# Attention logits finished on VectorE from head-major rows read back from DRAM, instead of by selector matmuls on TensorE

## The chip, the cores and the metric

The kernel runs on one core of a Trainium2 chip. The metric is device time in microseconds (us). Every profile is of one execution on the chip. TensorE is called PE in the profile, VectorE DVE, ScalarE ACT, GpSimd POOL; SP is the engine whose queue issues nearly all DMAs (all but two loads of `x` in the trace before).

A ratio of times is the mean time of one kernel's runs over the mean of the other's in the same rounds, so it is not quite the ratio of the medians that stand beside it. Brackets after a ratio are its 95% interval.

## The reference, cut to what matters

Two pairs of layers are applied to one sequence of 2048 tokens of width 1024. The first layer of a pair is sliding-window attention with 32 heads of 32 dimensions, 8 keys per query at a distance of 2 tokens. The second is a gated MLP of width 3584.

```
def _A_ref(x, wqkv, wo):
    B, S, D = x.shape
    H = 32; Dh = D // H
    W, dil = 8, 2
    qkv = (x @ wqkv).reshape(B, S, 3, H, Dh)              # (transposed; cut)
    ...
    logits = jnp.einsum("bhsd,bhswd->bhsw", q, kg) * scale
    logits = jnp.where(mask[None, None, :, :], logits, -1e9)
    attn = _softmax(logits, axis=-1)
    o = jnp.einsum("bhsw,bhswd->bhsd", attn, vg)
    return o.transpose(0, 2, 1, 3).reshape(B, S, D) @ wo

def _B_ref(x, W_gate, W_up, W_down):
    gate = jnp.einsum("bsd,df->bsf", x, W_gate)
    up = jnp.einsum("bsd,df->bsf", x, W_up)
    gate = gate * (gate > 0)
    return jnp.einsum("bsf,fd->bsd", gate * up, W_down)

# twice: x = x + A(layernorm(x)); x = x + B(layernorm(x))
```

## The kernel before

The tokens are cut into four pieces of 512, and with two pairs of layers that makes eight *blocks*, 0 to 7. TensorE runs one long stream of matmuls. Its *stage n* holds the 28 gate/up pairs of block n, then q and k of block n+2 (and v, in later stages), then the output projection of block n+1, then the down projection of block n. While TensorE is in the gate/up pairs of stage n, VectorE does the attention of block n+1: softmax, and a weighted sum of v in eight groups (`pv`).

VectorE has a second duty there. Each gate/up pair leaves two accumulators in PSUM. ScalarE empties the gate accumulator into `r`; VectorE empties the up accumulator with one multiplication, `hT <- acc_u, r`. That multiplication is called an *eviction* below, numbered from 1 to 28 within a stage, and so are the gates and ups. Six PSUM banks, of tag `acc`, serve all of these accumulators. If VectorE does something else for too long, TensorE finds no free bank (in the trace after, it waited up to 9.97 us for one).

The order of instructions on each engine, and which PSUM bank each accumulator gets, are fixed when the kernel is built. A scheduler chooses them, from its own model of how long things take and from the times (`at`) at which the program records each piece. The compute engines' order in the traces is the one that was built.

This is how an attention logit is made. VectorE multiplies q and k and adds up eight groups of dimensions into a tile `s`; each partition of `s` then holds a quarter of a head, that is, the sum over 8 of its 32 dimensions. To finish, four partitions have to be added. The kernel does it with a 0/1 selector matrix on TensorE, into two PSUM banks of their own (`L`):

```
def red_mm(n, prod, first, last):
    st = att[n]
    if first:
        st["L"] = psum_l.tile([P, W, P], F32, tag="L", name=f"L_{n}")
    with pe_group():
        for wh in range(2):
            for tq in range(TPB):
                mm(st["L"][32 * tq:32 * tq + 32, WH * wh:WH * (wh + 1), :], lhsT=sel[:],
                   rhs=prod[:, WH * wh:WH * (wh + 1), tq * P:(tq + 1) * P],
                   start=first, stop=last, skip_group_check=True, tile_position=(0, 32 * tq))
```

The softmax reads `L` from PSUM (the exponential in between is ScalarE's):

```
def softmax(n):
    st = att[n]
    Lt = st["L"]
    ... # mask of the first tokens
    nc.vector.tensor_reduce(m[:], Lt[:].rearrange("p w t -> p t w"), axis=AX.X, op=ALU.max)
    nc.vector.tensor_tensor(d[:], Lt[:], _ap(m, 0, [[0, W], [1, P]]), op=ALU.subtract)
    nc.scalar.activation(d[:], d[:], ACT.Exp, scale=scale)
    nc.vector.tensor_reduce(ssum[:], d[:].rearrange("p w t -> p t w"), axis=AX.X, op=ALU.add)
    ... # reciprocal rs, then a = d * rs
```

The gate/up step, with the eviction as its last line, and the recording of the events of a stage:

```
for nm in ("g", "u"):
    acc = psum.tile([P, BLK], F32, tag="acc", name=f"acc_{nm}")       # 6 banks
    ... # 8 matmuls
    if nm == "g":
        r = pool["hid"].tile([P, BLK], BF16, tag="r", name="r", bufs=3)
        tail_act[0] = nc.scalar.activation(r[:], acc[:], ACT.Relu).ins
nc.vector.tensor_tensor(hold["hT"][:, j, :], accs["u"][:], r[:], op=ALU.mult)

# in the loop over stages; `at` is the start of stage n
ev.append((at + 0.1, reds_n[n + 1]))                       # selectors of block n+1
ev.append((at + 0.2, lambda n=n: softmax(n + 1)))
spread(pv_steps(n + 1), at + 12.0, 6.5)
ev.append((at + 72.0, store_o(n + 1)))                     # attention output to DRAM,
ev.append((at + 72.1, load_o(n + 1)))                      # and back, transposed
```

Block 0 is handled apart and does not change. Block 1's selectors stand 58.1 us into stage 0, the other six blocks' at the start of their stage.

## Time and profile before

| | before |
|---|---|
| median of 4 runs (lowest to highest) | 1630.3 us (1630.06 to 1631.79) |
| span of the profiled execution | 1628.4 us |
| mean granted TensorE clock | 1.000 |

The first lines to read are the busy times of the engines, from the profile's first page: us, share of the span, and number of instructions.

```profile
PE 1618.6 (99%) x7589; PEld 782.2 (48%) x7638; DVE 1062.6 (65%) x926; ACT 506.1 (31%) x1050; POOL 255.7 (16%) x220
```

The list of waits of TensorE follows: what it was to compute, what it waited for, and the total us, the number of times and the longest.

```profile
PE scratch L129 <- DVE ones L296: 1.5, 1, 1.5
PE dacc L129 <- DVE x L700: 0.8, 1, 0.8
PE acc_v L129 <- DVE xnT_first L103: 0.6, 1, 0.6
PE tp L364 <- DVE xn_first L103: 0.4, 1, 0.4
```

TensorE is busy for all but 9.8 us and waits for 3.3. It is the bound: the only ways to be faster are fewer matmuls or cheaper ones, and any new wait of TensorE is a loss. The 65% of VectorE looks like plenty of room, but it is an average. In the stretch in which it begins block 1's attention it is full, as a line of the view by windows shows (columns: the window, its length, then busy us of PE, PEld, DVE, ACT and POOL, the granted clock, the DMA share and GB/s).

```profile
200.00:238.00 38.00, 38.00 (x180) 17.20 (x177) 36.87 (x38) 7.62 (x12) 0.00 (x0) 1.00 0.56 160
```

What the selectors cost is to be read from the timeline of TensorE at the start of stage 1 (start us, length us, engine, line, operation, out<-in, shapes, count):

```profile
330.57 1.89 PE L129 MATMUL acc_u<-xnT_b,w_u 128*128 128x512 bf16 x8
332.39 0.61 PE L129 MATMUL L<-s,sel 128*32 128x512 bf16 x8
332.94 1.90 PE L129 MATMUL acc_g<-xnT_b,w_g 128*128 128x512 bf16 x8
```

From the start of the up group to the start of the next gate group 2.37 us pass; an ordinary group of eight takes 1.73, so eight selector matmuls cost 0.64 us and not another 1.73. The program gives four of them different columns of the array (`tile_position`), and by their records those four run at once: four start at 332.39 us and the other four at 332.62.

And this is how VectorE mixes its two duties in stage 1: an eviction `hT` follows after every 2 to 5.5 us. The timeline of VectorE before:

```profile
333.18 1.21 DVE L565 TENSOR_REDUCE m<-L 128x128 f32<-128x1024 f32 x1
...
341.35 0.68 DVE L673 TENSOR_TENSOR hT<-acc_u,r 128x512 bf16<-128x512 f32 x1
341.95 4.48 DVE L603 TENSOR_TENSOR pv<-a,vhm 128x4096 bf16<-128x4096 bf16 x2
346.36 0.68 DVE L673 TENSOR_TENSOR hT<-acc_u,r 128x512 bf16<-128x512 f32 x1
```

### The profile page before, as it was taken

To read this page: it belongs to the slowest core of one execution; us is meant where nothing else is said; L and a number is where in the kernel's file an instruction comes from. 1 tells how busy PE (TensorE), PEld (TensorE's weight loads), DVE (VectorE), ACT (ScalarE), POOL (GpSimd) and SP (SyncE) were. 2 spreads that over 40 slices of the span, in tenths; PEclk is the share of its full clock that TensorE was granted. 3 is DMA by queue.
4 is the path that set the end of the run, shared out by engine and by line. 5 is a ranking of instruction groups with operands and counts; after the bars stand their busy time and mean duration, and the time that the engine had idled before them with its cause. 6 is when DMAs were issued, how large, how long until landed. Compare 5 with 4: busy or idle time off the path is not lost.

```text
span 1628.4 us, 18703 instructions
## 1 busy us (share of the span) xinstructions
PE 1618.6 (99%) x7589; PEld 782.2 (48%) x7638; DVE 1062.6 (65%) x926; ACT 506.1 (31%) x1050; POOL 255.7 (16%) x220
## 2 busy tenths in 40 slices
PE   9999999999999999999999999999999999999999
PEld 6644445444544445444454444544445444444444
DVE  5799899985497927949179492894818958211211
ACT  4754313243241513405134051331513311131110
POOL 2421003310250102201052010520105100000000
PEclk9999999999999999999999999999999999999999
DMA  9579656746476485664857647577484764655451
GB/s 303 93 203 252 167 177 199 192 156 200 136 215 175 155 233 171 184 175 150 229 181 185 187 150 225 162 203 212 151 231 154 194 205 155 206 164 172 156 168 65
DMA packets 371463, 296.83 MB, mean 182 GB/s; under 512 B 142512, under 2 KB 351664, under 8 KB 370480
## 3 DMA queue, kind: packets, MB, share of 16 engines
q1 hardware_dynamic: 371088, 295.23, 63.2%
q8 instruction: 60, 0.98, 0.3%
q10 hardware_dynamic: 288, 0.39, 0.1%
q14 instruction: 27, 0.22, 0.0%
HBM read 256.77 MB, written 21.00 MB: 171 GB/s over the span
## 4 chain that ended last, share of the span: by engine, by line
PE 95%; DVE 4%; issue 1%; DMA 0%; POOL 0%; DVEq 0%
PE acc_g L129 24%; PE acc_u L129 24%; PE dacc L129 22%; PE acc_v L129 7%; PE acc_k L129 6%; PE acc_q L129 6%; PE acc_wo L129 6%; DVE t L541 2%; DVE ac L551 1%; PE L L129 1%; DVE pv L603 0%; DVE x L648 0%; DVE pv L604 0%; DVE ac L541 0%; DMA x<-in_A_x_dram 0%
## 5 line engine op out<-in xcount | busy, mean ns | idle before, releaser
L129 PE MATMUL acc_g<-xnT_b,w_g 128*128 128x512 bf16 x1792 | 423.4, 379 | 0.0
L129 PE MATMUL acc_u<-xnT_b,w_u 128*128 128x512 bf16 x1792 | 423.3, 379 | 0.0
L129 PE MATMUL dacc<-w_d,hT 128*128 128x512 bf16 x1759 | 386.5, 379 | 2.5 <-DVE x L700 0.8
L672 ACT ACTIVATE r<-acc_g 128x512 bf16<-128x512 f32 x224 | 133.4, 596 | 747.1 <-PE acc_g L129 746.0
L673 DVE TENSOR_TENSOR hT<-acc_u,r 128x512 bf16<-128x512 f32 x224 | 153.7, 687 | 315.1 <-PE acc_u L129 313.5
L129 PEld LDWEIGHTS <-hT 128*128 128x128 bf16 x1792 | 175.4, 98 | 212.3 <-issue 1.0
L129 PEld LDWEIGHTS <-w_g 128*128 128x128 bf16 x1792 | 174.8, 98 | 212.7 <-issue 3.0
L129 PEld LDWEIGHTS <-w_u 128*128 128x128 bf16 x1792 | 175.4, 98 | 211.4
L541 DVE TENSOR_TENSOR t<-q,k 128x2048 f32<-128x2048 bf16 x84 | 191.7, 2290 | 8.6 <-ACT k L480 5.8
L551 DVE TENSOR_TENSOR ac<-ac,t 128x2048 f32<-128x2048 f32 x84 | 191.7, 2282 | 0.4
L485 POOL COPY kh<-k 128x14 bf16<-128x14 bf16 x64 | 81.2, 1273 | 471.9 <-ACT k L480 471.8
L700 DVE TENSOR_TENSOR x<-dacc,x 128x512 bf16<-128x512 f32 x64 | 42.5, 687 | 164.0 <-PE dacc L129 164.0
L603 DVE TENSOR_TENSOR pv<-a,vhm 128x4096 bf16<-128x4096 bf16 x64 | 145.2, 2282 | 0.0
L129 PE MATMUL acc_wo<-w_o,oT 128*128 128x512 bf16 x496 | 111.0, 379 | 0.8
L245 POOL TENSOR_TENSOR st_b<-st_b,neg_half 128x1 f32<-128x1 f32 x29 | 56.4, 1956 | 288.6 <-ACT st_b L244 288.6
L245 POOL TENSOR_TENSOR st_a<-st_a,neg_half 128x1 f32<-128x1 f32 x32 | 41.9, 1315 | 319.2 <-ACT st_a L244 319.1
L484 POOL COPY k<-kh 128x14 bf16<-128x14 bf16 x48 | 70.5, 1469 | 65.9 <-DVE t L541 43.8
L129 PEld LDWEIGHTS <-oT 128*128 128x128 bf16 x512 | 50.0, 98 | 60.4
L604 DVE TENSOR_TENSOR pv<-pv 128x2048 bf16<-128x2048 bf16 x64 | 77.4, 1215 | 0.2
L476 ACT CAST q<-acc_q 128x512 bf16<-128x512 f32 x64 | 37.3, 583 | 73.2 <-PE acc_q L129 73.2
L240 ACT ACTIVATE xn_b<-x 128x1024 bf16<-128x1024 bf16 x29 | 30.3, 1045 | 89.3 <-DVE x L648 89.3
L480 ACT CAST k<-acc_k 128x512 bf16<-128x512 f32 x64 | 37.3, 583 | 63.0 <-PE acc_k L129 62.8
(131 smaller groups left out, 1209.1 us busy)
## 6 DMA issues: line engine op xcount, KB each, us to landing
w_g<-in_B_W_gate_dram SPq DMA_DIRECT2D x56, 1024.0 KB, 7.0
w_u<-in_B_W_up_dram SPq DMA_DIRECT2D x56, 1024.0 KB, 5.4
w_d<-in_B_W_down_dram SPq DMA_DIRECT2D x48, 1024.0 KB, 5.8
w_o<-in_A_wo_dram SPq DMA_DIRECT2D x16, 1024.0 KB, 7.2
vhm<-v_d SPq DMA_DIRECT2D x32, 284.0 KB, 6.9
v_d<-vT SPq DMA_DIRECT2D x8, 1024.0 KB, 10.0
oT<-o_d SPq DMA_DIRECT2D x32, 256.0 KB, 4.4
w_d<-in_B_W_down_dram SPq DMA_DIRECT2D x16, 512.0 KB, 4.0
```

The costliest lines, as they stand in the source:

```text
L129: tail_pe[0] = nc.tensor.matmul(*args, **kwargs).ins
L245: nc.gpsimd.tensor_tensor(rstd, vpe, neg_half[:, 0:1], op=ALU.pow)
L476: tail_act[0] = nc.scalar.copy(q[:], acc[:]).ins
L484: nc.gpsimd.tensor_copy(k[:, 0:HALO], khalo[n - 1][:, c, :])
L485: nc.gpsimd.tensor_copy(khalo[n][:, c, :], k[:, BLK:BLK + HALO])
L541: nc.vector.tensor_tensor(t[:], i0, i1, op=ALU.mult)
L551: nc.vector.tensor_tensor(o, ac[:], t[:], op=ALU.add)
L603: nc.vector.tensor_tensor(tt[:], a_bc, v_sh, op=ALU.mult)
L604: nc.vector.tensor_tensor(tt[:, 0:4], tt[:, 0:4], tt[:, 4:8], op=ALU.add)
L672: tail_act[0] = nc.scalar.activation(r[:], acc[:], ACT.Relu).ins
L673: nc.vector.tensor_tensor(hold["hT"][:, j, :], accs["u"][:], r[:], op=ALU.mult)
L700: nc.vector.tensor_tensor(xs, ac[t], xs, op=ALU.add)
```

## The change

The intent is to take the 56 selector matmuls of blocks 1 to 7 off TensorE, the bound, and to use VectorE, which has idle time. `s` (1 MB) is stored to DRAM and read back in head-major order: 32 heads times 4 pieces of 128 tokens on the 128 partitions, with the four quarters of a head one after the other in the free dimension. Two additions on VectorE finish the logits. The pieces read are 256 bytes each. Because the trip takes time, the softmax and everything behind it are recorded later. The two `L` banks are now free in the down projection, and its second half uses them. The core of the diff:

```
-        def red():
-            red_mm(n, st["s"], True, True)
+    def store_s(n):
+        def f():
+            sp_dma(s_d[n % 2][:], att[n]["s"][:].rearrange("p w t -> p (w t)"))
+        return f
+
+    def load_s(n):
+        def f():
+            sd = s_d[n % 2]
+            s4 = work.tile([P, DG, W, P], BF16, tag="t", name=f"s4_{n}")
+            for tq in range(TPB):
+                src = bass.AP(tensor=sd.tensor, offset=sd.offset + tq * P,
+                              ap=[[DG * W * BLK, H], [BLK, DG * W], [1, P]])
+                sp_dma(s4[32 * tq:32 * tq + 32, :, :, :].rearrange("p d w t -> p (d w) t"), src)
+            att[n]["s4"] = s4
+        return f
+
+    def head_sum(n):
+        s4 = att[n].pop("s4")
+        u = work.tile([P, DG // 2, W, P], F32, tag="ac", name=f"u_{n}", bufs=1)
+        nc.vector.tensor_tensor(u[:], s4[:, 0:2], s4[:, 2:4], op=ALU.add)
+        nc.vector.tensor_tensor(u[:, 0], u[:, 0], u[:, 1], op=ALU.add)
+        return u[:, 0]
 
     def softmax(n):
         st = att[n]
-        Lt = st["L"]
+        Lt = st["L"] if n == 0 else head_sum(n)
 ... (down projection, second half)
+                    own = TPB if half == 0 else TPB // 2
+                    accs[half] = [psum.tile([P, BLK], F32, tag="acc", name=f"dacc{t}")[:] for t in range(own)]
+                    if half == 1:
+                        pair = psum_l.tile([P, TPB // 2, BLK], F32, tag="L", name="dacc_pair")
+                        accs[half] += [pair[:, t, :] for t in range(TPB // 2)]
 ... (block 1)
-    ev.append((t_gu0 + 58.1, red1))
-    ev.append((t_gu0 + 58.2, lambda: softmax(1)))
+    ev.append((t_gu0 + 51.0, store_s(1)))
+    ev.append((t_gu0 + 56.0, load_s(1)))
+    ev.append((t_gu0 + 61.0, lambda: softmax(1)))
 ... (block 1's pv at +66.5; its output is stored in three parts, at +90, +101, +108; blocks 2 to 7:)
-            ev.append((at + 0.1, reds_n[n + 1]))
-            ev.append((at + 0.2, lambda n=n: softmax(n + 1)))
-            spread(pv_steps(n + 1), at + 12.0, 6.5)
-            ev.append((at + 72.0, store_o(n + 1)))
+            ev.append((at - 2.0, store_s(n + 1)))
+            ev.append((at + 3.0, load_s(n + 1)))
+            ev.append((at + 9.0, lambda n=n: softmax(n + 1)))
+            spread(pv_steps(n + 1), at + 21.0, 6.5)
+            ev.append((at + 80.0, store_o(n + 1)))
```

The instruction orders of the two built kernels could be compared before anything ran. That comparison gives the places in VectorE's order that the prediction speaks of.

More of the change, by code (lines that the diff above doesn't have):

```diff
@@ L156 @@
     o_d = dram.tile([NT, H, DH, P], BF16, name="o_d")
+    s_d = [dram.tile([P, W * BLK], BF16, name=f"s_d{i}") for i in range(2)]
     zpad = const.tile([P, KC, HALO], BF16, name="zpad")
@@ L551, in add @@
             nc.vector.tensor_tensor(o, ac[:], t[:], op=ALU.add)
-        def red():
-            red_mm(n, st["s"], True, True)
-        return [mult(h, c) for h in range(2) for c in range(KC)], red
+        return [mult(h, c) for h in range(2) for c in range(KC)]
+    def store_s(n):
[18 more added lines that the diff above has]
+        return u[:, 0]
     def softmax(n):
         st = att[n]
-        Lt = st["L"]
+        Lt = st["L"] if n == 0 else head_sum(n)
         if n % NB == 0:
@@ L564, in softmax @@
         m = soft.tile([P, P], F32, tag="m", name="m")
-        nc.vector.tensor_reduce(m[:], Lt[:].rearrange("p w t -> p t w"), axis=AX.X, op=ALU.max)
+        nc.vector.tensor_reduce(m[:], (Lt[:] if n == 0 else Lt).rearrange("p w t -> p t w"), axis=AX.X, op=ALU.max)
         d = soft.tile([P, W, P], F32, tag="d", name="d")
-        nc.vector.tensor_tensor(d[:], Lt[:], _ap(m, 0, [[0, W], [1, P]]), op=ALU.subtract)
+        nc.vector.tensor_tensor(d[:], Lt[:] if n == 0 else Lt, _ap(m, 0, [[0, W], [1, P]]), op=ALU.subtract)
         nc.scalar.activation(d[:], d[:], ACT.Exp, scale=scale)
@@ L685, in f @@
                 if s8 == 0:
-                    accs[half] = [psum.tile([P, BLK], F32, tag="acc", name=f"dacc{t}")[:] for t in range(TPB)]
+                    own = TPB if half == 0 else TPB // 2
[3 more added lines that the diff above has]
+                        accs[half] += [pair[:, t, :] for t in range(TPB // 2)]
                 ac = accs[half]
@@ L724 @@
     ln_b = {}
-    reds_n = {}
     ln_a[0] = ln_first()
@@ L795 @@
     ev.append((t_wo0 + 3.0, store_v(2)))
-    sums1, red1 = prod_sum_steps(1)
+    sums1 = prod_sum_steps(1)
     spread(sums1[:4], t_qk1 + 50.0, 4.4)
@@ L814 @@
         if n == 0:
-            spread(pv_steps(1), at + 66.0, 5.5)
-            ev.append((at + 105.0, store_o(1)))
-            ev.append((at + 105.1, load_o(1)))
-        elif n + 1 < NN:
-            ev.append((at + 0.1, reds_n[n + 1]))
-            ev.append((at + 0.2, lambda n=n: softmax(n + 1)))
-            spread(pv_steps(n + 1), at + 12.0, 6.5)
-            ev.append((at + 72.0, store_o(n + 1)))
-            ev.append((at + 72.1, load_o(n + 1)))
+            spread(pv_steps(1), at + 66.5, 5.5)
+            ev.append((at + 90.0, store_o(1, 0, 4)))
+            ev.append((at + 101.0, store_o(1, 4, 6)))
+            ev.append((at + 108.0, store_o(1, 6, 8)))
+            ev.append((at + 108.1, load_o(1)))
+        elif n + 1 < NN:
+            ev.append((at - 2.0, store_s(n + 1)))
[3 more added lines that the diff above has]
+            ev.append((at + 80.0, store_o(n + 1)))
+            ev.append((at + 80.1, load_o(n + 1)))
         if n + 2 < NN:
@@ L829 @@
             spread(qk_steps(n + 2, ln_a[n + 2], ("qk", n + 2)), at, GRP)
-            sums, reds_n[n + 2] = prod_sum_steps(n + 2)
-            spread(sums, at + GRP * (K_STEP[0] + 1.0), 4.4)
+            spread(prod_sum_steps(n + 2), at + GRP * (K_STEP[0] + 1.0), 4.4)
             at += 2 * GRP * KC
```

## The prediction

> What bounds it now. The profile's busy table gives TensorE 1618.6 of 1628.4 us; the list of waits gives TensorE only 3.3 us of waits. VectorE is busy 65%, but in the timeline from 200 to 323 us (softmax, weighted sum of block 1, product sums of block 2) it is full: 36.9 of 38 us, then 27.9 of 28. The clock is 1.0 throughout. So time is TensorE's matmul stream (0.216 us per 128x512 matmul, 3.455 us per gate/up pair) plus any wait put into it.
>
> Removed: 56 selector matmuls. Each group of eight moves the stream by about 0.64 us (timeline, 330.57 to 332.94 us, less one group of eight), because four use different column groups at once[...]. Seven groups: 4.5 us, all critical.
>
> Added, per block: a 1 MB store (like o_d, landed in about 4 to 10 us), four 256 KB reads in 256-byte pieces (4.4 us each for oT), and on VectorE a bf16-to-fp32 add of 2048 (2.2 us, as t<-q,k) and an fp32 add of 1024 (1.2 us, as d): 3.4 us. [...]here bf16 2048 takes 1.22 us, fp32 2.28.
>
> Moved, and this decides it: the static order on VectorE. Each head sum stands behind gate/up eviction 8 of 28 (blocks 2 to 7; softmax used to stand behind the first) and 24 (block 1; was 17), as if the scheduler took the DMA round trip for much slower than I expect. It then runs long stretches with no eviction (hT<-acc_u,r): in block 1 head sum, softmax and four weighted-sum groups, about 28.4 us; in blocks 2 to 7 about 10.8 us between evictions 10 and 11. TensorE has six accumulators and cannot wait that long.
>
> Hand arithmetic over the queues, with durations from the trace:
> - Block 1: eviction 24 at 224 us, 25 only at 253. TensorE stops near 244 (k of block 2 needs eviction 25's bank), resumes at 254 to 260, then waits for block 1's attention output, whose last group ends near 281 instead of 251; store and reload put the output projection at about 288 instead of 266. Loss 21 to 23 us.
> - Blocks 2 to 7: gate 15 waits about 3.4 us for eviction 11, gate 17 about 2.4 us for eviction 13: 5.8 us each, 35 us in all.
> The two extra PSUM banks in the second half of the down projection take away at most about 1 us of waits.
>
> Sum: 1630 - 4.5 + 22 + 35 = 1682 us. Range 1655 to 1702. Faster by over 2%: 0.02; within 2%: 0.16; slower: 0.82.
>
> What would show it: TensorE waits in the gate/up stage named after hT or x; a TensorE gap near 244 to 254 us and another before the first acc_wo after it, ended by DMA oT; in blocks 2 to 7 two gaps near 48 and 58 us into each gate/up stage; VectorE idle from about 191 to 224 us but for evictions; head sum 2.2 and 1.2 us; no L<-s; TensorE busy still near 1614 us; DMA waits on the head-major tile near zero (data lands about 10 us after the stage starts, used at 28).
>
> What would make it wrong: if banks or the r tiles free earlier than the built order's waits say, or VectorE runs the chain faster in SBUF than from PSUM, the small gaps (35 us) shrink and the result is within 2%. If the 256-byte reads are far slower than oT's, weights queue behind them and it is worse.

## The result and the profile after

| | before | after |
|---|---|---|
| median of 4 runs (lowest to highest) | 1630.3 us (1630.06 to 1631.79) | 1690.2 us (1688.88 to 1690.43) |
| ratio | | 1.0364 [1.0346, 1.0382] |
| span of the profiled execution | 1628.4 us | 1688.7 us |
| span less TensorE's busy time | 9.8 us | 53.8 us |
| mean granted TensorE clock | 1.000 | 0.986 |

The results are correct. The kernel became 3.6% slower; the span grew by 60.3 us. The busy times of the engines after:

```profile
PE 1634.9 (97%) x7582; PEld 784.8 (46%) x7582; DVE 1092.1 (65%) x940; ACT 503.2 (30%) x1050; POOL 262.6 (16%) x220
```

In the trace before, 49 matmul records are missing (7589 matmuls for 7638 weight loads), so the counts of PE cannot be compared; those of the weight loads (PEld) can, and they are 56 fewer, one for each selector matmul.

The 60.3 us split into 44.0 of TensorE not busy (53.8 less 9.8) and 16.3 of TensorE busy longer (1634.9 less 1618.6), although it has fewer matmuls to do. The five longest entries of the list of waits of TensorE after (four more, of 1.5 us and less, are left out):

```profile
PE acc_g L129 <- DVE hT L694: 21.6, 7, 4.3
PE acc_k L129 <- DVE hT L694: 10.0, 1, 10.0
PE acc_u L129 <- DVE hT L694: 5.1, 4, 2.1
PE acc_k L129 <- DMA w_('qk', 2)_k<-in_A_wqkv_dram: 4.1, 1, 4.1
PE acc_wo L129 <- DMA oT<-o_d: 3.6, 1, 3.6
```

Three of the five name an eviction. None names the tile that came back from DRAM.

A table by stage says where it was lost. A stage is measured from the start of its first gate group to the start of the next stage's, in both traces; the attention of block n+1 runs in stage n.

| stage (block in attention) | before | after | difference |
|---|---|---|---|
| 0 (1) | 188.06 | 210.88 | +22.8 |
| 1 (2) | 187.13 | 193.18 | +6.1 |
| 2 (3) | 200.94 | 206.98 | +6.0 |
| 3 (4) | 200.95 | 207.71 | +6.8 |
| 4 (5) | 200.94 | 206.98 | +6.0 |
| 5 (6) | 200.95 | 207.91 | +7.0 |
| 6 (7) | 159.50 | 164.26 | +4.8 |

Block 1 costs 22.8 us and blocks 2 to 7 together 36.6. What comes before and after these stages adds the rest.

**Block 1.** The timeline of TensorE after; the brackets give the idle time ahead of a group and what ended it.

```profile
254.85 1.87 PE L129 MATMUL acc_k<-xnT_a,w_('qk', 2)_k 128*128 128x512 bf16 x4 [9.97 <-DVE hT L694]
...
288.21 15.67 PE L129 MATMUL acc_wo<-w_o,oT 128*128 128x512 bf16 x64 [3.61 <-DMA oT<-o_d]
```

TensorE stands still for 10 us up to 254.85, again for 4.14 us up to 260.86 (a DMA of weights), and for 3.61 before the output projection. The timeline of VectorE shows what it did in the meantime:

```profile
224.33 0.69 DVE L694 TENSOR_TENSOR hT<-acc_u,r 128x512 bf16<-128x512 f32 x1 [2.76 <-PE acc_u L129]
224.93 2.28 DVE L575 TENSOR_TENSOR u<-s 128x2048 f32<-128x2048 bf16 x1
227.25 1.23 DVE L576 TENSOR_TENSOR u<-u 128x1024 f32<-128x1024 f32 x1
228.51 1.91 DVE L586 TENSOR_REDUCE m<-u 128x128 f32<-128x1024 f32 x1
...
253.44 0.75 DVE L627 TENSOR_TENSOR ohm<-pv 128x512 bf16<-128x512 bf16 x2
254.12 1.28 DVE L694 TENSOR_TENSOR hT<-acc_u,r 128x512 bf16<-128x512 f32 x2
```

From 224.93 to 254.12 us there is not one eviction: head sum, softmax and four groups of the weighted sum stand in a row. Eviction 25, at 254.12, is what TensorE's k waited for. VectorE idled ahead of eviction 24, so it was not late with other work; it was told to do this here.

The 4.14 us wait for a weight slab is a matter of order too, on another queue. The timeline of SP's queue:

```profile
254.22 0.34 SPq L118 DMA_DIRECT2D o_d<-ohm  x1
254.66 0.39 SPq L118 DMA_DIRECT2D w_('qk', 2)_k<-in_A_wqkv_dram  x1
```

The store of the first half of the attention output waits for VectorE, and the weights stand behind it in the same queue, which kept its order: from 224.62 to 254.22 us it issued nothing, 29.5 us of that waiting for `ohm`, and the weights followed 0.44 us after the store.

The three waits must not be added up, though. What the projection waits for is the attention output, and its last piece comes from VectorE's queue. After:

```profile
280.18 2.29 DVE L542 TENSOR_TENSOR t<-q,k 128x2048 f32<-128x2048 bf16 x1 [0.22 <-POOL k L485]
282.39 0.42 DVE L627 TENSOR_TENSOR ohm<-pv 128x512 bf16<-128x512 bf16 x1
```

and before, with the projection:

```profile
250.74 0.41 DVE L606 TENSOR_TENSOR ohm<-pv 128x512 bf16<-128x512 bf16 x1
265.77 13.98 PE L129 MATMUL acc_wo<-w_o,oT 128*128 128x512 bf16 x62
```

From 224.93 to 282.81 us VectorE had only two gaps in the trace after: 1.12 us for ScalarE's exponential and 0.22 us for k. So the two waits of k cost about 0.2 us by this trace; had k come earlier, the projection would have waited longer instead. The projection started 147.03 us into the stage, 22.05 later than before (124.98); its matmuls took 1.7 us longer (15.67 against 13.98); and the free PSUM banks gave back 0.9 us in this stage (e7_pair, below). Together these are the 22.8 us.

**Blocks 2 to 7.** TensorE in stage 1 (block 2), which started at 352.06 us:

```profile
398.68 1.89 PE L129 MATMUL acc_u<-xnT_b,w_u 128*128 128x512 bf16 x8
404.61 3.40 PE L129 MATMUL acc_g<-xnT_b,w_g 128*128 128x512 bf16 x8 [4.03 <-DVE hT L694]
407.80 2.10 PE L129 MATMUL acc_u<-xnT_b,w_u 128*128 128x512 bf16 x8
409.74 1.89 PE L129 MATMUL acc_g<-xnT_b,w_g 128*128 128x512 bf16 x8
...
414.02 1.89 PE L129 MATMUL acc_g<-xnT_b,w_g 128*128 128x512 bf16 x8 [0.66 <-DVE hT L694]
```

And VectorE up to the eviction that ended the wait:

```profile
392.52 0.68 DVE L694 TENSOR_TENSOR hT<-acc_u,r 128x512 bf16<-128x512 f32 x1
393.12 4.48 DVE L624 TENSOR_TENSOR pv<-a,vhm 128x4096 bf16<-128x4096 bf16 x2
397.53 2.35 DVE L625 TENSOR_TENSOR pv<-pv 128x2048 bf16<-128x2048 bf16 x2
399.80 1.28 DVE L626 TENSOR_TENSOR pv<-pv 128x1024 bf16<-128x1024 bf16 x2
401.00 0.75 DVE L627 TENSOR_TENSOR ohm<-pv 128x512 bf16<-128x512 bf16 x2
401.67 2.28 DVE L624 TENSOR_TENSOR pv<-a,vhm 128x4096 bf16<-128x4096 bf16 x1
403.88 0.68 DVE L694 TENSOR_TENSOR hT<-acc_u,r 128x512 bf16<-128x512 f32 x1
```

Compare the piece shown of before: there an eviction stood on both sides of each pair of `pv`; here, between eviction 10 (at 392.52) and eviction 11 (at 403.88), two whole groups and a third multiplication run. Gate 15 needs the bank that eviction 11 frees, and starts 0.05 us after its end.

Stages 2 to 4 have this order too. In stages 5 and 6 (blocks 6 and 7) the built order was another one: no eviction stood inside the softmax, and the two groups ran between evictions 9 and 10. TensorE's waits there were 1.34, 3.81 and 0.37 us in stage 5, and 1.32 and 2.08 in stage 6.

The gate group after the 4.03 us gap took 3.40 us instead of 1.89. The windows show why; the column to read is the granted clock, third from the end:

```profile
406.00:407.50 1.50, 1.50 (x5) 0.58 (x4) 1.50 (x3) 1.50 (x4) 0.00 (x0) 0.50 0.00 0
409.00:412.00 3.00, 3.00 (x16) 1.37 (x14) 3.00 (x4) 0.67 (x3) 0.00 (x0) 1.00 0.00 0
```

The granted clock was 0.50 from 406.00 to 407.50 us, behind the 4.03 us of idling, and 1.00 again from 409.00 to 412.00.

So the first reading is this. In blocks 2 to 7 no wait of TensorE names the trip: the data for block 2 was asked for at 359.09 us, a read of 256 KB took 6.8 us (median, four at once), and the tile was used at 380.57. What hurts is the place at which VectorE's softmax and weighted sum were put, and above all which evictions stand between their pieces.

### The profile page after: what moved, and what is told of

It reads as the page before. It is cut to its first block, busy times and chain, and to the rows that moved or that the text cites. A ratio compares the mean times of both kernels' runs of the same rounds, so it can differ in the third digit from the quotient of the medians.

```text
span 1688.7 us, 18704 instructions
## 1 busy us (share of the span) xinstructions
PE 1634.9 (97%) x7582; PEld 784.8 (46%) x7582; DVE 1092.1 (65%) x940; ACT 503.2 (30%) x1050; POOL 262.6 (16%) x220
## 4 chain that ended last, share of the span: by engine, by line
PE 85%; DVE 11%; issue 1%; POOL 1%; DMA 1%; ACT 0%; DVEq 0%; SPq 0%
PE acc_u L129 19%; PE acc_g L129 19%; PE dacc L129 17%; PE acc_wo L129 7%; PE acc_v L129 7%; PE acc_k L129 6%; PE acc_q L129 6%; PE dacc_pair L129 6%; DVE pv L624 3%; DVE pv L625 1%; POOL kh L486 1%; DVE u L575 1%; DVE ssum L591 1%; DVE m L586 1%; DVE hT L694 1%
## 5 line engine op out<-in xcount | busy, mean ns | idle before, releaser
L129 PE MATMUL acc_g<-xnT_b,w_g 128*128 128x512 bf16 x1792 | 431.7, 385 | 21.7 <-DVE hT L694 21.6
L129 PE MATMUL dacc<-w_d,hT 128*128 128x512 bf16 x1344 | 295.3, 379 | 0.0
L486 POOL COPY kh<-k 128x14 bf16<-128x14 bf16 x64 | 97.4, 1527 | 430.4 <-ACT k L481 430.2
L725 DVE TENSOR_TENSOR x<-dacc,x 128x512 bf16<-128x512 f32 x48 | 31.4, 686 | 160.1 <-PE dacc L129 160.1
L129 PE MATMUL dacc_pair<-w_d,hT 128*128 128x512 bf16 x448 | 101.9, 379 | 0.0
L246 POOL TENSOR_TENSOR st_b<-st_b,neg_half 128x1 f32<-128x1 f32 x29 | 47.6, 1651 | 287.9 <-ACT st_b L245 287.9
```

What stands on the lines that cost most here:

```text
L129: tail_pe[0] = nc.tensor.matmul(*args, **kwargs).ins
L246: nc.gpsimd.tensor_tensor(rstd, vpe, neg_half[:, 0:1], op=ALU.pow)
L486: nc.gpsimd.tensor_copy(khalo[n][:, c, :], k[:, BLK:BLK + HALO])
L725: nc.vector.tensor_tensor(xs, ac[t], xs, op=ALU.add)
```

## The experiments

The theory tested is that the *order*, of VectorE's evictions and of SP's queue, makes the loss. Its rivals are *work* (W: two additions per block, 3.5 us of VectorE, are too much for a full engine) and the *DRAM trip* (D: stores, reads and their traffic cost time, whatever the order). Ten kernels ran; each is compared with runs of the kernel before on the same chip. Kernels are compared only within the same rounds. All gave correct results.

| run | us | before, same rounds | ratio [95%] |
|---|---|---|---|
| e1_pin27 | 1652.56 | 1630.78 | 1.0127 [1.0112, 1.0142] |
| e2_pinall | 1649.29 | 1630.78 | 1.0110 [1.0094, 1.0125] |
| e3_work | 1630.40 | 1630.78 | 0.9996 [0.9981, 1.0011] |
| e4_order_work | 1657.51 | 1630.78 | 1.0159 [1.0142, 1.0176] |
| e5_best | 1626.17 | 1630.14 | 0.9975 [0.9962, 0.9987] |
| e6_sel2 | 1633.20 | 1630.14 | 1.0018 [1.0005, 1.0030] |
| e7_pair | 1629.82 | 1630.14 | 0.9997 [0.9984, 1.0009] |
| e8_fill | 1698.06 | 1630.14 | 1.0416 [1.0400, 1.0432] |
| e9_trip | 1692.68 | 1630.13 | 1.0382 [1.0366, 1.0397] |
| e10_pinall2 | 1638.33 | 1630.13 | 1.0054 [1.0037, 1.0070] |

### e1_pin27: the changed kernel with VectorE's order fixed, blocks 2 to 7

The change keeps its trip and its additions. In stages 1 to 6 the evictions, softmax and weighted sum of VectorE are chained, so that the scheduler has to keep the order in which they are recorded; the softmax is split in two events and recorded later, where the program can place evictions between the pieces.

```
+    def gv(pin, f, *args, **kwargs):
+        with (tc.issue_after(tail_gu[0]) if pin and tail_gu[0] is not None else nullcontext()):
+            ins = f(*args, **kwargs).ins
+        if pin:
+            tail_gu[0] = ins
+        return ins
 ... (every VectorE call of head_sum, softmax, pv and the eviction goes through gv(n >= 2, ...))
-            ev.append((at + 9.0, lambda n=n: softmax(n + 1)))
-            spread(pv_steps(n + 1), at + 21.0, 6.5)
-            ev.append((at + 80.0, store_o(n + 1)))
+            ev.append((at + 22.0, lambda n=n: softmax_a(n + 1)))
+            ev.append((at + 26.0, lambda n=n: softmax_b(n + 1)))
+            spread(pv_steps(n + 1), at + 32.0, 6.5)
+            ev.append((at + 88.0, store_o(n + 1)))
```

> The changed kernel with one edit: in blocks 2 to 7 VectorE's instructions of the gate/up stage are pinned so that an eviction (hT) stands between any two weighted-sum groups and inside the softmax; same work, same DRAM round trip, block 1 untouched. Theory O (static order of VectorE): the six stages lose nothing any more, 1690.2 - 36.6 (sum of the six lengthened block periods, 6.05+6.04+6.76+6.04+6.96+4.76) - 3.8 (six selector groups at 0.64, now really saved) = about 1650 us, range 1647 to 1656; TensorE waits for hT in those stages under 1 us in all. Rival W (VectorE has about 4 us more work per block): unchanged, 1685 to 1691. Rival D (DMA round trip or its contention slows the weights): unchanged or nearly, over 1680.

It took 1652.56 us, inside the range expected. Waits for evictions in stages 1 to 6 are gone altogether; each of these stages now takes between 0.65 us less and 0.42 us more than before, while stage 0 still loses 23.1. The same additions and the same trip, in another order, cost nothing in blocks 2 to 7. Both W and D fall for these blocks.

### e2_pinall: block 1 too

```
+    ev.append((t_gu0 + 66.5, lambda: softmax_a(1)))
+    ev.append((t_gu0 + 70.0, lambda: softmax_b(1)))
 ...
+            spread(pv_steps(1), at + 77.0, 4.9)
+            ev.append((at + 96.5, store_o(1, 0, 4)))
+            ev.append((at + 106.5, store_o(1, 4, 6)))
+            ev.append((at + 116.0, store_o(1, 6, 8)))
 ... (gv now for blocks 1 to 7)
```

> As e1, and block 1 pinned as well (head sum behind eviction 20 instead of 24, weighted sums interleaved). Theory O: block 1 loses only what the later arrival of its logits pushes behind: attention output ends about 10 us later than before the change, so the output projection waits some 0 to 6 us; total 1624 to 1640 us, middle 1630. Rivals W and D: block 1 still loses about 23 us, total no lower than e1 (1650).

It missed: 1649.29 us. Stage 0 still loses 19.2 us. The wait of k for eviction 25 is gone, and two others stand in its place:

```profile
PE acc_k L138 <- DMA w_('qk', 2)_k<-in_A_wqkv_dram: 10.0, 1, 10.0
PE acc_wo L138 <- DMA oT<-o_d: 7.3, 1, 7.3
```

My own store had done the first: SP's queue issued it at 246.59 and the weight slab behind it at 247.02. The second came from VectorE: the first products of block 2 were free to go ahead of the last two groups of the weighted sum, so the attention output was finished at 278.6 us instead of 251.2. The experiment did not say what the trip costs in block 1; e10_pinall2 was built for that.

### e3_work: the two additions alone

To the kernel before, the two additions are added in each block's softmax, on data at hand, and their result is not used.

```
         Lt = st["L"]
+        if n > 0:
+            sw = st["s"][:].rearrange("p w (a t) -> p w a t", t=P)
+            u = work.tile([P, DG // 2, W, P], F32, tag="ac", name=f"u_{n}", bufs=1)
+            nc.vector.tensor_tensor(u[:].rearrange("p d w t -> p w d t"), sw[:, :, 0:2], sw[:, :, 2:4], op=ALU.add)
+            nc.vector.tensor_tensor(u[:, 0], u[:, 0], u[:, 1], op=ALU.add)
```

> The kernel before plus only the added VectorE work: per block 1 to 7 the two adds (128x2048 bf16 to fp32, 128x1024 fp32) on data already on chip, result unused; selectors stay. Theory O: the adds fall into VectorE's idle time or push it a little where it is full (block 1): 1630 to 1636 us. Rival W: 7 x 3.5 us = +24, 1654 us.

It took 1630.40 us, ratio 0.9996 with 1 well inside the interval. Rival W by itself is out: 3.5 us more VectorE work per block costs nothing where the scheduler still places evictions between the pieces.

### e4_order_work: the order with the two additions, without the trip

The kernel before, selectors and all, without a trip, but with the evictions, softmax and weighted sum of blocks 2 to 7 chained into the order that the changed kernel had got in stages 1 to 4 (softmax behind eviction 8, two groups and a third multiplication between evictions 10 and 11, and so on), and with the two additions.

```
+            ev.append((at + 2 * GRP * 7.4, lambda n=n: softmax_a(n + 1)))
+            ev.append((at + 2 * GRP * 8.4, lambda n=n: softmax_b(n + 1)))
+            for k, f in pv_ordered(n + 1):
+                ev.append((at + 2 * GRP * (k - 0.6), f))
+            ev.append((at + 80.0, store_o(n + 1)))
 ... (pv_ordered: the same eight groups, in pieces, each placed behind the eviction that it had in the changed kernel)
```

> The kernel before with VectorE's gate/up stage of blocks 2 to 7 pinned into the very order that the changed kernel got (softmax behind eviction 8, two weighted-sum groups without an eviction), plus the two adds there; no DRAM trip, selectors stay. In the built order the PSUM banks are handed out differently from the changed kernel: up 15 and up 17 (not gate 15 and gate 17) wait for evictions 11 and 13, 1.73 us more slack. Theory O with banks as a part of it: stalls of about 1 to 2 us per block, 1636 to 1646 us. If the order alone decides whatever the banks: about 5 us per block, 1660 to 1668. Rival D (the trip is needed for the loss): 1630 to 1633.

It took 1657.51 us, between what the two variants of the theory expected. The order with the additions, without one byte through DRAM, makes each of stages 1 to 6 lose 4.2 to 5.8 us, through one line of the waits:

```profile
PE acc_u L138 <- DVE hT L109: 23.4, 12, 2.3
```

There are two waits per stage: of up 15 for eviction 11 (1.50 us in stage 1), and of up 17 for eviction 13 (2.34 us). The stage that lost 5.8 is stage 5, where the matmuls behind the second wait ran slowly (3.06 us for a group of eight). In the changed kernel gate 15 waited for that same eviction 11. The eviction comes at the same time in both: 51.7 us into the stage here, 51.8 after. But the banks had been handed out differently, and here the one needed is asked for one group later. That is 1.73 us, and the selectors put TensorE's stream 0.64 us later: 2.4 us of the 2.5 by which the changed kernel's stage 1 loses more (6.7 with the 0.64 us of its removed selectors put back, against 4.2). So the loss has two static parts: VectorE's order, and which bank the next group was given. The order was not run without the additions. They stand between evictions 8 and 9, in a stretch of VectorE's queue whose only gap (0.53 us, for the exponential) lies behind them, so by an estimate from this trace their 3.5 us are most of the 3.84 us that the two waits take. What e3_work and e4_order_work show together is that this order makes work critical which is free in another. That an order can cost time without any added work is what e9_trip shows.

### e5_best: what remains if the order is right

Block 1 keeps the selectors; blocks 2 to 7 use the trip with the order of e1_pin27. The store of the attention output is moved behind the weight slab of k, which e1_pin27 had still waited for by 0.8 us at most.

```
-    sums1 = prod_sum_steps(1)
+    sums1, red1 = prod_sum_steps(1)
 ... (block 1's events as before the change; softmax reads st["L"] if n < 2)
-            ev.append((at + 88.0, store_o(n + 1)))
+            ev.append((at + (98.2 if n + 2 < NN else 84.0), store_o(n + 1)))
```

> Candidate: block 1 finished by selector matmuls as before the change, blocks 2 to 7 by the DRAM trip and VectorE with the pinned order of e1, and the store of the attention output put behind the second k slab in the DMA queue (in e1 it stood ahead of it and cost 0.3 to 0.8 us in four blocks). Theory O: six selector groups saved and nothing given back: 1630.8 - 6 x 0.64 = 1627 us, ratio 0.997 to 0.999. If head sums on VectorE or the trip cost anything, even well ordered: at or over 1631.

It took 1626.17 us (1625.98 to 1626.82), against 1630.14 (1630.04 to 1632.04): 0.9975 [0.9962, 0.9987]. This beats both kernels, and lies in the range expected. The trace's spans differ by 3.3 us; of TensorE's waits only those up to the first gate group are left. Each of the stages 1 to 5 is about 0.65 us shorter, which is one group of selectors. A part of the gain is that of the two extra banks, which this kernel keeps (stage 0 is 0.93 us shorter, as in e7_pair); against e7_pair it is 3.65 us, or 0.61 for each of the six groups. The change's intent was right for blocks 2 to 7, then, and worth that much: a quarter of a per cent.

### e6_sel2: the selectors' cost, by doubling them

```
             red_mm(n, st["s"], True, True)
+            red_mm(n, st["s"], False, True, True)      # the same eight again, into the same L
```

> The kernel before with each selector group of blocks 1 to 7 issued twice (the second writes the same sums again); measures what the change could gain. Each group moves the matmul stream by 0.64 us: +4.5 us, 1635 us. If the groups run one after another at 0.216 us a matmul it would be 8 x 0.216 x 7 = +12 us; if they hide behind other work, 0.

It took 1633.20 us, 3.06 more than before: 0.44 us for each of the seven added groups. The two groups run as one, in TensorE's timeline:

```profile
333.37 1.05 PE L129 MATMUL L<-s,sel 128*32 128x512 bf16 x16
```

The added group costs two matmul times (2 × 0.216 = 0.43 us): eight matmuls, four at once. The first group costs 0.64, 0.2 us more; no run shows where these 0.2 us come from.

### e7_pair: the free PSUM banks in the down projection, alone

```
+                    own = TPB if half == 0 else TPB // 2
 ... (as in the change's diff; selectors stay)
```

> The kernel before with only the PSUM part of the change: two of the four accumulators of the second down half in the banks of L. All theories: removes the one wait of 0.8 us for x in block 2's stage, nothing else: 1629 to 1631 us.

It took 1629.82 us; the 0.8 us wait of `dacc` for `x` is gone, stage 0 is 0.93 us shorter, and the other stages are as before. The ratio's interval holds 1, so a gain is seen in the trace and not established in the time.

### e8_fill: is the half clock part of the loss?

After the 4.03 us gap TensorE ran at half its clock (0.50 granted). If that is a loss of its own, then keeping TensorE busy through the gap must win it back; if VectorE's order is what binds, it must not matter. The changed kernel got 18 matmuls of no use in front of gate 15 in stages 1 to 5.

```
+                if j == 14 and 1 <= n <= 5:
+                    scratch(18)
```

> The changed kernel with 18 scratch matmuls (3.9 us) put into the gap of about 4 us ahead of gate 15 in five stages (blocks 2 to 6), so that TensorE stays busy there and its granted clock should not fall to 0.5 after it. If the slow clock after the gap (1.5 to 2 us of slower matmuls each) adds to the loss: 1680 to 1683 us. If VectorE's queue sets the time through eviction 13 (gate 17 then just waits longer): the second wait grows from 0.7 to about 2.2 us and the time stays at 1687 to 1691.

The total, 1698.06 us, is outside both expectations. In stage 5 the gaps lay elsewhere (1.33 us and 3.81 us, ahead of the filler), so there the filler was 3.6 us of extra work; stages 3 and 4 lost 1.3 and 1.7 more. In stages 1 and 2 the test is clean. TensorE in stage 1 there:

```profile
400.48 4.05 PE L129 MATMUL scratch<-ones 128*128 128x512 bf16 x18
404.68 1.89 PE L129 MATMUL acc_g<-xnT_b,w_g 128*128 128x512 bf16 x8 [0.15 <-DVE hT L696]
...
414.09 1.89 PE L129 MATMUL acc_g<-xnT_b,w_g 128*128 128x512 bf16 x8 [2.33 <-DVE hT L696]
```

Gate 15 ran at full speed (1.89 us), and gate 17 then waited 2.33 us instead of 0.66. The stage took 193.18 us with the filler and 193.18 without; stage 2 took 206.99 and 206.98. The slow matmuls of blocks 2 and 3 cost nothing: they only filled time in which VectorE's queue was not yet as far as eviction 13. Stages 3 and 4 show the other side. There the wait of gate 17 was itself followed by slow matmuls:

```profile
814.55 3.02 PE L129 MATMUL acc_g<-xnT_b,w_g 128*128 128x512 bf16 x8 [2.34 <-DVE hT L696]
```

Behind it came no further wait that could absorb them, and these are the stages that took 1.3 and 1.7 us longer. So in stages 1 and 2 slow matmuls cost nothing ahead of the next wait for an eviction; behind the last such wait, in stages 3 and 4, they made a gate/up pair 1.7 us longer (5.14 us instead of 3.455).

### e9_trip: the round trip alone, order left to the scheduler

The kernel before, with its selectors, and with the store of `s` and the four reads recorded where the change records them; the reads land in a second DRAM tensor and nobody waits for them.

```
+    r_d = dram.tile([P, DG * W * P], BF16, name="r_d")
 ... (store_s and load_s as in the change, but with r_d in place of s4)
+    ev.append((t_gu0 + 51.0, store_s(1)))
+    ev.append((t_gu0 + 56.0, load_s(1)))
+            ev.append((at - 2.0, store_s(n + 1)))
+            ev.append((at + 3.0, load_s(n + 1)))
```

> The kernel before plus only the DRAM round trip (same store, same 256-byte reads, but landing in a second DRAM tensor[...], and read by nobody); selectors, VectorE's work and all its data dependences as before. Built, VectorE's order changes although nothing on it depends on the trip: in blocks 2 to 7 there are 17 us of weighted sums without an eviction (8 to 9), and gate 13 waits for eviction 9. Theory O (the scheduler believes the trip to hold back the weights and orders by that): waits named hT, about 6.5 us per block at 42 us into the stage, plus some 1.5 us of slow clock: 1670 to 1690 us. If the trip itself is what costs (contention, weights late): waits named DMA of a weight tile. If neither: 1630.

It took 1692.68 us, slightly more than expected and as bad as the whole change, although no instruction uses what the trip brings. There are no waits of TensorE for weights. It waits for evictions, 47.8 us in these two lines:

```profile
PE acc_g L129 <- DVE hT L689: 25.5, 4, 6.4
PE acc_u L129 <- DVE hT L689: 22.3, 3, 9.6
```

In stage 1, for example, VectorE has no eviction from 362.90 to 379.92 us, because the scheduler put several groups of the weighted sum in one row there; gate 13 waits 6.36 us for the eviction that follows. No wait in the stages names a DMA, and VectorE has no added work here: what costs is the order that came of recording the trip. The loss lies in other places than in the changed kernel, though (3.2 us in stage 0, 8 to 12 in each of stages 1 to 6), so this run shows that two of the change's lines are enough to spoil the order, and not that they spoil it in the same way.

### e10_pinall2: block 1 with both orders mended

As e2_pinall, with block 1's output stored behind the second half of the k weights, the groups of the weighted sum closer together, and the first product of block 2 held back until they are done.

```
-                if n == 1:
+                if n == 1 or (n == 2 and h == 0 and c == 0):
 ...
+            spread(pv_steps(1), at + 77.0, 3.6)
+            ev.append((at + 98.2, store_o(1, 0, 4)))
+            ev.append((at + 99.5, store_o(1, 4, 6)))
+            ev.append((at + 103.0, store_o(1, 6, 8)))
```

> e2 mended in block 1: the first store of attention output goes behind the second k slab in the DMA queue (in e2 that slab waited 10 us behind it), all weighted sums of block 1 go ahead of the product sums of block 2 on VectorE, and the stores of blocks 2 to 7 stand as in e5. Expected by theory O: no wait for the k slab; attention output of block 1 ends near 265 us (251 before the change), the output projection waits about 6 to 7 us for it (plus about 2 us of slow clock); total 1631 to 1637 us. If block 1's loss has another cause: 1645 or more.

It took 1638.33 us, just above the range. Waits for evictions and for weights are gone. Stages 1 to 5 are 0.65 us shorter than before; stage 0 loses 11.5 us, or 12.1 with the 0.64 of its selectors put back. One wait stands out, in TensorE's timeline:

```profile
273.65 16.04 PE L138 MATMUL acc_wo<-w_o,oT 128*128 128x512 bf16 x64 [8.39 <-DMA oT<-o_d]
```

Three parts make up 11.7 of the 12.1 us: 8.4 of waiting for the attention output; 2.1 because the 64 matmuls behind that wait were slower (16.04 us; the same matmuls took 13.98 before); and 1.2 by which a wait of the down projection for `x`, right behind, grew (1.99 us; 0.76 before). So of the 22.8 us that block 1's stage lost in the changed kernel about half were order, and half are left with VectorE's order and SP's mended. VectorE's was not mended to the end: only the first product of block 2 was held back, and another one (2.28 us, at 263.31) still ran ahead of the sums of the last group, so up to 2.2 us of the 8.4 are order too. The attention output was finished at 267.9 us, 16.8 later than before; 10.3 of these are the later start (head sum at 210.72, softmax before at 200.38), 3.5 the additions and 0.7 the reduction. Block 1's softmax is recorded 8.3 us later than before in this kernel, in a stretch in which VectorE is full. Whether an earlier trip would win the rest back was not tried.

## Why the prediction was right or wrong

The prediction was 1682 us (1655 to 1702) with 0.82 for slower by over 2%; the result is 1690.2 us. It was right in direction, mechanism and range, and 8 us low. Term by term:

- **"Removed ... 4.5 us, all critical": right.** e5_best shows 0.65 us for each stage whose selectors went away. e6_sel2 shows that doubling them costs less (0.44 us per group); why was not shown. I had put 4.5 us on that too, and it was 3.06.
- **"Added ... 3.4 us" of VectorE work: right, and harmless in itself.** 2.28 + 1.23 us in the trace; e3_work shows no cost. In the changed kernel's order they stand ahead of the evictions that TensorE waits for, and there they count.
- **"Moved, and this decides it": right.** e1_pin27 takes the loss of blocks 2 to 7 away by order alone; e4_order_work makes most of it by that order and the additions, without the trip. That the scheduler took the trip for slower than it is remains an argument: e9_trip shows that recording the trip is enough to change the order, not what the scheduler had assumed.
- **Block 1, "21 to 23 us": right.** TensorE stopped at 244.9 and resumed at 254.85, waited again up to 260.86, and started the output projection at 288.21 (about 288 was predicted). The stage lost 22.8 us, or 23.5 with the selectors' 0.64 put back. That 288 was met so well is partly luck: the last group ended at 282.8 (281 predicted), and store and reload took 5.4 us instead of 7. The trace adds two things that I had not separated: the weight slab of k behind a waiting store, which cost about 0.2 us, and the slow matmuls behind a long gap, 1.7 us.
- **Blocks 2 to 7, "5.8 us each, 35 us in all": right in kind, too small.** This is the term that was mis-sized. Measured are 6.1, 6.0, 6.8, 6.0, 7.0 and 4.8 us per stage; with 0.64 for the removed selectors put back, 6.7 us on average and 40.4 in all. The single waits fell otherwise than predicted, and in blocks 6 and 7 other groups waited than gates 15 and 17. In stage 1 gate 15 waited 4.03 us (3.4 predicted), gate 17 0.66 (2.4 predicted), and between them the groups ran 1.7 us slower (5.13 us from gate 15 to gate 16, an ordinary pair taking 3.455). Their sum, 6.4 us, is what counts, and e8_fill shows for blocks 2 and 3 that the slow clock only stands in for a part of the second wait. What made the sum larger is VectorE's own chain. Among what could make it wrong I had listed that "VectorE runs the chain faster in SBUF than from PSUM". The opposite happened: the maximum over the logits took 1.91 us from SBUF and 1.21 from PSUM (the same fp32 reduction over 8 values 512 bytes apart, 1024 values per partition in both; means of 7 and 8 instructions). The sum over the exponentials, with the same steps and in SBUF in both kernels, took 1.90 and 1.92 us (medians before and after). Why the two sources differ was not shown. Those 0.7 us stand ahead of eviction 11, in a stretch of the queue whose only gap lies behind them, and the first wait exceeded its prediction by 0.6. In e4_order_work, where the same pieces run with the reduction from PSUM, the way from eviction 8 to eviction 11 takes 23.10 us (stage 1, start to start), against 23.92 after. For six blocks 0.7 us are an estimated 4.2 us of the 5.4 us by which the term was short; no run took that reduction back to PSUM with all else equal, so this share was worked out and not shown by itself.
- **"The two extra PSUM banks ... at most about 1 us": right** (e7_pair, 0.3 us, within the noise).
- **"DMA waits on the head-major tile near zero": right.** There are none.
- **"TensorE busy still near 1614 us": wrong.** It was 1634.9, since matmuls behind gaps of 3.6 to 10 us, and behind one of 2.08, ran in part at half the clock (0.50 granted). A gap of about 2 us did not always end so: behind the one of 2.08 us, which ended at 1425.16, eight matmuls took 3.37 us, but of the six gaps of 2.34 and 2.35 us in e4_order_work five were followed by groups of 1.89 us and one by slow matmuls (3.06 us for a group). I had not thought of the clock. It made nothing of the loss in blocks 2 and 3, as e8_fill shows, but it is real in block 1, where 64 matmuls of the output projection took 15.7 us instead of 14.0 (mean granted clock 0.89 instead of 1.00).

The sum as measured: −4.5 (selectors) + 23.5 (block 1) + 40.4 (blocks 2 to 7) + 0.9 (before the first and behind the last of these stages) = 60.3 us.

## What to carry to other kernels

Where a static schedule feeds accumulators to a saturated TensorE, the order of the engine that empties them is part of the change: count how long it goes without an eviction, against the banks that TensorE has, before counting the work added. Recording a DMA trip in front of a softmax saved 4.5 us of selector matmuls and lost 65; in six of the seven blocks, chaining evictions between the pieces kept the saving and removed the loss. When several waits follow one another, ask which one ends last: the earlier ones may cost nothing (in e8_fill a stage took 193.18 us with the slow matmuls and 193.18 without). And in a queue that keeps its order, as SP's did here, a store that waits for a slow engine must not stand ahead of weights that TensorE will need (10.0 us of waiting in e2_pinall).
